# Contiguous Fourier products, an unread tile dropped and a new instruction plan in a fused attention and Fourier kernel

## The chip, the cores and the metric

The kernel runs on one core of one Trainium2 chip. The metric is the time of one execution on the device, in microseconds (us). One execution per kernel was also recorded by the profiler; its span, from the first to the last recorded instruction, is one or two us shorter than its time. A run is counted as slow when it is over 1.5% above the fastest run of the same kernel, and as fast otherwise; comparisons here are between fast runs. The engines are called as the profile calls them: PE is TensorE's matmuls and PEld its weight loads, DVE is VectorE, ACT ScalarE, POOL GpSimd, and SP the engine that issues the DMAs here.

## The reference, cut to what matters

```python
# x: 2048 x 640, 32 heads of 20, 4 segments of L = 512 tokens
q, k, v = x @ wq, x @ wk, x @ wv
for s in range(4):
    p   = softmax(q_s @ k_s^T * scale + mask)         # causal inside the segment
    num = phi(q_s) @ M;  den = phi(q_s) @ z           # memory of the segments before; M = 0 in segment 0
    o_s = g * num/den + (1 - g) * (p @ v_s)
    M += phi(k_s)^T @ v_s;  z += sum(phi(k_s))
a = o @ wo
b = irfft2(rfft2(x) * (w_r + 1j * w_i))               # over tokens and channels
return gate * a + (1 - gate) * b                      # gate = sigmoid(sum(x * gate_w))
```

phi(t) is t + 1 for positive t and exp(t) otherwise. The memory is empty in segment 0, so nobody needs phi(q) there; the full-array copy of q that phi reads is made per segment and 128-channel tile.

## The kernel before

The kernel does not fix the order of its instructions in its source. It makes some 2,350 operations, each with the buffers it reads and writes and with an assumed duration, and a list scheduler, run when the kernel is built, simulates them, picks for each engine the ready operation of the lowest priority number, and so fixes what each engine executes and in which order. On the chip every engine executes its list in that order: two profiles of the kernel after, `after` and `after_again`, show the same 3,243 matmuls in the same sequence. `PLAN` is a tuple of one correction to the priority per group of operations, found by a search against that same simulation. The chip never sees the simulated times, only the order. We call the simulation the model, and a time that it gives a planned time; none of these is a measurement.

The D products (a real Fourier transform over the channels, as matmuls with cosine and sine tables) write the even and odd frequencies to every other column of one PSUM bank, and one copy takes the bank to SBUF as `Bt`:

```python
# typ 0: cosines, typ 1: sines; (source block, first PSUM column, stride, columns, table column)
parts = ((0, 0, 2, 161, 0), (1, 0, 1, KD, 161), (2, 1, 2, 160, 482)) if typ == 0 else (
    (2, 1, 2, 160, 642), (3, 0, 1, KD, 802), (4, 0, 2, 161, 1123))          # KD = 321
for n_, (c, c0, st, n, tc) in enumerate(parts):
    ... matmul(ps(bank, c0, [st, n]), Ac[c], big[tc:tc+n], start=n_ == 0, stop=n_ == 2)
copy_alts(Bt.ap(typ * 322, [1, KD]), ps(bank, 0, [1, KD]))                   # on ACT or DVE
```

For each of 12 output tiles (segments 0 to 2, four each) the attention result `o`, which had been stored to the scratch `o_scr`, is loaded back transposed into one of four buffers `oT`, multiplied with `wo` on top of the gated Fourier part (`Fb`), copied to `ot` and stored. All these loads and stores are issued by SP, in one order:

```python
k4 = self.finc % 4                                  # four buffers oT, taken in turn
self.dma(oT[k4], o_scr tile, tr=True, name="oT")    # transposing load, 160 KB; waits for the buffer's last reader
for hf in range(2):
    self.mms(Fb ...)                                # gate * Fourier part, 32-row tiles of the array
    self.mms(5 products wo, oT ..., name="oproj")   # 320 columns each
    self.Sc.op(copy to ot ..., name="final")
self.dma(out tile, ot, name="st_out")
```

## Time and profile before

The median of the first three runs was 256.04 us (255.94 to 256.11). The first two lines below, from the top of the page, give the span and each engine's busy time, share of the span and number of instructions; then come the page's picture of the span in 40 equal slices (busy tenths of PE and of the granted clock), and the chain of waits that ended last, as shares of the span by engine.

```profile
span 255.2 us, 7980 instructions
PE 241.7 (95%) x3248; PEld 142.3 (56%) x3248; DVE 203.2 (80%) x556; ACT 202.8 (79%) x208; POOL 114.2 (45%) x175
...
PE   7999989997999999989989999999998999999994
PEclk9999997999999999999999999999999999999999
...
PE 78%; DVE 7%; DMA 5%; ACT 3%; SPq 2%; issue 1%; POOL 1%; ACTq 0%; DVEq 0%
```

PE is never idle for long, 78% of the chain is PE work, and the clock dips once (the 7 in `PEclk`). The waits of PE, in total us, number and longest, from the view of waits:

```profile
PE psum L590 <- DVE va L1086: 1.6, 1, 1.6
PE psum L590 <- DVE qu L600: 1.6, 3, 0.8
```

From the starts of neighbouring matmuls in the trace one can divide PE's time (249.7 us between its first and its last matmul) into four terms: plain work at the rate of undisturbed neighbours, 96 ns for each change of array mode, the excess inside stretches of half clock, and the rest, which is waits and slow steps. The division is the author's estimate; how much it puts down to half clock depends on whether the slow steps of PE at the start are counted, as they are here.

| between first and last matmul, us | before |
|---|---|
| plain steps | 204.1 |
| 208 changes of array mode | 20.0 |
| half clock | 4.1 |
| rest (waits, slow D steps) | 21.6 |

This agrees with what the Trainium skill says in "TensorE: Matmul & The Clock Gate", section "Back-to-back issue gap", for a step (columns / 2.4 + 2.5 ns, which the page calls the gap of an isolated matmul): the trace has 216 ns for 512 columns, 135 for 320 and 56 for 128.

### The profile page before, as it was taken

Reading aid. Unit: us, or ns where it says so; the run is one execution under the profiler, and the core shown is the slowest. Engines: PE = TensorE matmul, PEld = TensorE weight load, DVE = VectorE, ACT = ScalarE, POOL = GpSimd, SP = SyncE. Lnnn points to the kernel's source line nnn. Section 1 sums busy time; section 2 is a strip of 40 time slices with the busy share of each in tenths; the row PEclk is TensorE's granted clock in tenths of the full one; section 3 lists DMA queues with packets and bytes.
Section 4 is the critical chain, followed back from the end, with each engine's and each line's share of the span. In section 5 each row is a group of like instructions: output and inputs, shape, how many; then the busy total and the mean of one; then the engine's idle time right before and its main releaser. Section 6 shows DMA issues by size and latency. Waiting matters only on the chain.

```text
span 255.2 us, 7980 instructions
## 1 busy us (share of the span) xinstructions
PE 241.7 (95%) x3248; PEld 142.3 (56%) x3248; DVE 203.2 (80%) x556; ACT 202.8 (79%) x208; POOL 114.2 (45%) x175
## 2 busy tenths in 40 slices
PE   7999989997999999989989999999998999999994
PEld 2344556554666657644655566545564656456583
DVE  0799897768888999899999988989999984625543
ACT  2397599877899998999988889889889798788710
POOL 8015634433532346745255748434665432416400
PEclk9999997999999999999999999999999999999999
DMA  7996979499449356746247484213565303553223
GB/s 181 362 356 189 214 165 238 104 216 225 125 79 243 98 142 187 164 143 172 58 103 177 110 207 104 89 44 113 123 167 167 66 3 81 91 115 96 74 72 103
DMA packets 56003, 36.76 MB, mean 144 GB/s; under 512 B 31792, under 2 KB 52256, under 8 KB 55968
## 3 DMA queue, kind: packets, MB, share of 16 engines
q1 hardware_dynamic: 54272, 35.45, 55.1%
q10 hardware_dynamic: 1696, 0.82, 1.2%
q8 instruction: 25, 0.41, 0.7%
q14 instruction: 10, 0.08, 0.1%
HBM read 19.86 MB, written 9.84 MB: 116 GB/s over the span
## 4 chain that ended last, share of the span: by engine, by line
PE 78%; DVE 7%; DMA 5%; ACT 3%; SPq 2%; issue 1%; POOL 1%; ACTq 0%; DVEq 0%
PE psum L590 78%; DMA pkn<-phk 3%; ACT ex L1180 2%; SPq L619 2%; DVE Pt L1329 2%; DMA tt<-tab_tt 1%; DMA kp<-k_scr 1%; DVE va L1086 1%; DVE mem L1123 1%; POOL Yt L1334 1%; DVE Cp L600 1%; DVE G L1375 1%; ACT eo L598 1%; DVE qu L600 1%; POOL ex L1183 1%
## 5 line engine op out<-in xcount | busy, mean ns | idle before, releaser
L1180 ACT ACTIVATE ex<-psum 128x2048 bf16<-128x2048 f32 x80 | 150.3, 1879 | 19.2 <-PE psum L590 18.7
L1183 POOL TENSOR_SCALAR_AFFINE_SELECT ex<-ex 128x512 bf16<-128x512 bf16 x128 | 80.7, 648 | 111.3 <-ACT ex L1180 108.8
L590 PEld LDWEIGHTS psum<-va,ex 128*128 128x128 bf16 x1280 | 36.7, 96 | 6.7 <-issue 1.5
L590 PE MATMUL psum<-va,ex 128*128 128x21 bf16 x1280 | 38.6, 172 | 1.0 <-POOL ex L1183 0.3
L590 PE MATMUL psum<-qp,kp 20*128 20x512 bf16 (+3 forms) x512 | 31.9, 303 | 1.4 <-DMA kp<-k_scr 0.8
L590 PE MATMUL psum<-xT,wk 128*128 128x512 bf16 (+1 forms) x140 | 28.6, 381 | 1.3 <-DVE qu L600 0.8
L590 PE MATMUL psum<-xT,wq 128*128 128x512 bf16 (+1 forms) x140 | 28.3, 381 | 0.2 <-DVE Pt L1329 0.2
L590 PE MATMUL psum<-wv,xT 128*128 128x141 bf16 (+1 forms) x160 | 28.0, 306 | 0.0
L1329 DVE TENSOR_TENSOR Pt<-psum,Wt 128x642 bf16<-128x642 f32 x32 | 25.6, 821 | 2.1 <-PE psum L590 1.9
L590 PE MATMUL psum<-wo,oT 128*128 128x320 bf16 x120 | 22.1, 301 | 0.0
L590 PEld LDWEIGHTS psum<-qp,kp 20*128 20x128 bf16 x512 | 8.9, 92 | 21.4 <-ACT ex L1180 9.3
L590 PE MATMUL psum<-big,Ac 128*128 128x161 bf16 (+2 forms) x96 | 18.6, 316 | 0.7 <-DVE qu L600 0.6
L590 PEld LDWEIGHTS psum<-wv,xT 128*128 128x128 bf16 x160 | 13.2, 99 | 9.2 <-issue 1.2
L590 PE MATMUL psum<-big,Cp 128*128 128x321 bf16 (+1 forms) x96 | 17.2, 302 | 1.0 <-DVE eo L600 0.4
L1051 ACT ACTIVATE et<-qu 128x512 bf16<-128x512 bf16 x25 | 15.6, 630 | 2.7 <-DVE qu L600 2.5
L1086 DVE TENSOR_TENSOR va<-psum,ebx 128x500 bf16<-128x500 f32 (+1 forms) x32 | 15.2, 481 | 3.2 <-PE psum L590 2.3
L600 DVE CAST ot<-psum 128x320 bf16<-128x320 f32 x19 | 9.1, 490 | 10.6 <-PE psum L590 9.5
L590 PEld LDWEIGHTS psum<-xT,wk 128*128 128x128 bf16 (+1 forms) x140 | 9.8, 98 | 12.9 <-issue 2.2
L1375 DVE TENSOR_TENSOR G<-eo,psum 128x320 bf16<-128x320 f32 x32 | 14.6, 475 | 2.5 <-PE psum L590 2.4
L590 PEld LDWEIGHTS psum<-xT,wq 128*128 128x128 bf16 (+1 forms) x140 | 10.3, 98 | 11.2 <-issue 1.6
L1215 DVE TENSOR_TENSOR on<-psum,rs 128x320 bf16<-128x320 f32 x32 | 15.4, 482 | 0.3
L590 PE MATMUL psum<-tt,Yt 128*128 128x256 bf16 (+1 forms) x96 | 15.3, 276 | 0.1
(80 smaller groups left out, 360.0 us busy)
## 6 DMA issues: line engine op xcount, KB each, us to landing
tt<-tab_tt SPq DMA_DIRECT2D x16, 256.0 KB, 3.0
xsb<-in_A_x_dram SPq DMA_DIRECT2D x8, 320.0 KB, 6.8
qp<-q_scr SPq DMA_DIRECT2D x28, 80.0 KB
kp<-k_scr SPq DMA_DIRECT2D x28, 80.0 KB
o_scr<-on SPq DMA_DIRECT2D x12, 160.0 KB
out_dram<-ot SPq DMA_DIRECT2D x12, 160.0 KB
q_scr<-qu SPq DMA_DIRECT2D x6, 256.0 KB
k_scr<-qu SPq DMA_DIRECT2D x6, 256.0 KB, 2.8
```

Of the source, the lines that this page charges most:

```text
L590: h = e.matmul(o_, l_, r_, start=st, stop=sp_, **kw)
L598: alts["act"] = (lambda e: e.activation(dst(), src(), ACT.Copy), 100 + 0.833 * n, 95.0)
L600: alts["dve"] = (lambda e: e.tensor_copy(dst(), src()), 75 + 1.04 * n, 85.0)
L619: return e.dma_start(d_, s_)
L1051: self.one("act", lambda e: e.activation(et.ap(0, [1, L]), qsl(), ACT.Exp), L, [qb], [b("et", pi_)], late, name="phi_exp")
L1086: self.one("dve", lambda e: e.tensor_tensor(va.ap(i * H * VW + h0 * VW, [VW, nh], [1, DH]), self.ps(bank, 0, [DH, nh], [1, DH]), self.ebx. ...
L1123: self.one("dve", lambda e: e.tensor_tensor(self.mem.ap(i * D + q * 320, [DH, 16], [1, DH]), self.ps(bank, 0, [VW, 16], [1, DH]), dn.ap(16 ...
L1180: self.one("act", lambda e: e.activation(dst(), src(), ACT.Exp, scale=SC), 4 * width, [bank], [self.exb(s, g, j) for g, j in outs], prio - ...
L1183: self.one("pool", lambda e, g=g, j=j: e.affine_select(self.ex.ap(self.exo(s, g) + JOFF[j], [1280, 4], [1, P]), self.ex.ap(self.exo(s, g) ...
L1215: self.one("dve", lambda e, rs=rs, bank=bank, g=g: e.tensor_tensor(on.ap(80 * g, [D, 4], [DH, 4], [1, DH]), self.ps(bank, 0, [88, 4], [VW, ...
L1329: self.one("dve", lambda e, ri=ri, Pt=Pt, Wt=Wt, bank=bank: e.tensor_tensor(Pt.ap(ri * 322, [644, 2], [1, KD]), self.ps(bank, 0, [0, 2], [ ...
L1375: self.one("dve", lambda e, q=q, n2=n2, bank=bank, eo=eo: e.tensor_tensor(self.G.ap(n2 * D + 639 * q, [1 - 2 * q, 320]), eo.ap(q, [1, 320] ...
```

## The change

The intent: D products that write contiguous PSUM columns (odd frequencies first, then even ones, with the interleaving left to the copy that leaves PSUM), no q tile 0 in segment 0, which nobody reads, and a new plan, searched with a model that knows changes of array mode and has newly measured durations. The diff, cut to its core:

```diff
@@ the D products @@
-                parts = ((0, 0, 2, 161, 0), (1, 0, 1, KD, 161), (2, 1, 2, 160, 482)) if typ == 0 else (
-                    (2, 1, 2, 160, 642), (3, 0, 1, KD, 802), (4, 0, 2, 161, 1123))
+                parts = ((0, 160, 161, 0), (1, 0, KD, 162), (2, 0, 160, 484)) if typ == 0 else (
+                    (2, 0, 160, 644), (3, 0, KD, 804), (4, 160, 161, 1126))
-                        return (self.ps(bank, c0, [st, n]), ...
+                        return (self.ps(bank, c0, [1, n]), ...
-    copy_alts(Bt.ap(typ * 322, [1, KD]), ps(bank, 0, [1, KD]), KD)
+    copy_alts(Bt.ap(typ * 322 + 1, [-1, 2], [2, 161]), ps(bank, 0, [160, 2], [1, 161]), 322)
@@ the dropped tile @@
     def proj_tile(self, s, which, t, prio, xT, xb):
+        if s == 0 and which == "q" and t == 0:
+            return
@@ the scheduler's model @@
+    SWITCH = 95.0
+                    if o.mode != pe_mode:
+                        occ += self.SWITCH
+                        pe_mode = o.mode
-PECOL = 0.43
+PECOL = 1.0 / 2.4
-        cost = 700.0 + nbytes / 260.0 if tr else 580.0 if nbytes in (41088, 163840) else 430.0
+        cost = 740.0 + nbytes / 262.0 if tr else self.ISSUE.get(name, 450.0)
-        xfer = nbytes / row * (9.0 + row / 26.3) / 16 * 1.15
+        xfer = nbytes / row * (9.0 + row / 26.3) / 16 * 1.288
     ... (fixed parts and latencies of ACT, DVE and POOL work likewise)
     PLAN = ( ... every number replaced ... )
```

The remaining lines move table columns by a few places and pass the array mode to the model.

## The prediction

> **What bounds the kernel now.** TensorE. The page's first part has PE busy 241.7 of 255.2 us (95%), the two eviction engines 80% and 79%. The chain of waits is 78% PE. By stretches, PE has no gap from 200 to 245 us; from 100 to 200 us it is 95% busy and VectorE 93%. I take start-to-start times of neighbouring matmuls in the trace: a 512-column one takes 216 ns, 320 columns 135, 128 columns 56. That agrees with the Trainium skill, "TensorE: Matmul & The Clock Gate", section "Back-to-back issue gap" (columns / 2.4 + 2.5 ns). With such steps, 25 ns for the 21-column ones and 96 ns per change of array mode (below), PE's work adds up to about 224 us. The rest of the 249.7 us between its first and last matmul is some 3.3 us of half-speed warm-up, 3.0 us of slow D products, and about 19 us of waits, a half-clock window of 3.4 us among them.
>
> **What the change does to PE.**
> 1. D products. Today two of three write PSUM with a stride of two. The trace shows steps of 96, 178 and 96 ns for 161, 321 and 160 columns; at the rate of all other matmuls they would be 69, 136 and 69. The 321 one writes contiguously, so I read its 178 as backlog of the strided one ahead (once, with other matmuls between, it took 147). Contiguous halves save about 95 ns x 32 = 3.0 us. The eviction now interleaves on its way out; from PSUM it took 488 ns on VectorE and 442 ns on ScalarE, and I expect no more than 10% on that.
> 2. Dropped q tile: 5 x 216 = 1.1 us of PE, one ScalarE eviction (0.6 us), 128 KB of store.
> 3. Array modes. Going between full array and 32-row or 32-column tiles costs 94 to 101 ns over the plain step (317 against 216, 229 against 135, 152 against 56). The Trainium skill says that a change of mode drains the array ("TensorEngine Tiling (Array Packing)", "Key Properties"); the trace agrees. The trace has 208 changes, the built order of the changed kernel 191. 17 x 96 ns = 1.6 us.
>
> Together 5.7 us of PE work. Almost all of it lies on the chain; but D lies where VectorE is 93% busy, and VectorE's load barely falls (Yt sums and additions go to GpSimd, q and k evictions come: about -1 us, from built counts and durations). So 1 us may come back as waits.
>
> 4. The new plan, from a model with measured costs, should cut waits: the largest (1.6 us before a T product at 59 us, 0.8 at 38 and 111, eight over 0.3) are of the kind that a plan moves. I give it -2 us, uncertain by 3 either way; it may equally make or remove a half-clock window (1.7 us).
> The phi maximum: VectorE has it in both builds (30 operations, 281 to 380 ns), so nothing.
>
> **Sum.** 256.0 - 5.7 + 1.0 - 2.0 = 249.3 us, range 246.0 to 252.5.
>
> **What would show it.** D steps of 69, 136, 69 ns; 191 mode changes at about 96 ns; xT,wq full-array matmuls 95 in place of 100; Bt evictions still about 490 and 440 ns; waits of PE 16 to 19 us.
>
> **What would make it wrong.** D products slow because of accumulation over part-written columns, not stride; a strided eviction write costing much; the plan overfitted to its model, so that PE waits for loads or VectorE grow by over 3 us, or a second half-clock window.

## More of the kernel before

The groups that the change and the argument touch: D products, output products, then the copies of D to `Bt` on the two engines (count, then minimum, median and maximum duration in ns), and, of the tile `oT`, what PE and PEld sat idle for before the output products that read it (us, times), with the time of its loads from issue to landing. The last line covers only the loads whose landing the view can pair with their issue, 7 of the 12 here and 3 of the 12 in the kernel after:

```profile
L590 PE MATMUL psum<-big,Ac 128*128 128x161 bf16 (+2 forms) x96 | 18.6, 316 | 0.7 <-DVE qu L600 0.6
L590 PE MATMUL psum<-wo,oT 128*128 128x320 bf16 x120 | 22.1, 301 | 0.0
L600 DVE CAST Bt<-psum x17: 478/485/497, 50.0 to 170.2; 128x321 bf16<-128x321 f32 x17
L598 ACT ACTIVATE Bt<-psum x15: 435/442/453, 74.7 to 165.6; 128x321 bf16<-128x321 f32 x15
...
  issue: 1.1, 5
...
DMA to landing us min/median/max: 2.8/3.0/3.9
```

The idle time of PE before all 120 output products is 0.0 us, and no part of PEld's idle time is put down to an `oT` load: the loads had landed before they were needed. By the semaphores that all 12 loads raise, they took 2.75 to 5.47 us, 3.1 in the median.

## The result, and the profile after

The changed kernel's median was 267.7 us (266.17 to 269.02, four runs), beside 256.08 us of the kernel before on the same chip (255.94 to 257.31). The ratio is 1.0449, with a 95% interval of 1.0402 to 1.0496. All ratios here are the mean time of one kernel's fast runs over that of the other's of the same rounds, so they are not quite the ratios of the medians quoted. Against the predicted 249.3 us the kernel is slower, and 15 us above the upper end of the range.

Here are the same lines of the page for the kernel after:

```profile
span 264.4 us, 7987 instructions
PE 242.0 (92%) x3243; PEld 139.1 (53%) x3243; DVE 202.5 (77%) x552; ACT 203.3 (77%) x208; POOL 115.0 (44%) x178
...
PE   7869999899999999899989899999999799798994
PEclk9968999999999999999999979999999899889999
...
PE 47%; DVE 22%; DMA 16%; SPq 7%; ACT 4%; issue 3%; POOL 0%; ACTq 0%; DVEq 0%
```

The largest of its waits of PE, with the one for the table of the D products:

```profile
PE psum L600 <- DMA oT<-o_scr: 4.3, 3, 1.7
PE psum L600 <- ACT ex L1200: 3.6, 4, 2.0
...
PE psum L600 <- DMA big<-tab_big: 1.3, 1, 1.3
```

PE has the same busy time as before, but only 47% of the chain of waits is PE, with DVE, DMA and the SP queue in its place. `PEclk` has dips near the start, at about 155 us and twice near the end; by the records of the granted clock they are half-clock stretches of 6.8 us from 14.6 us on, and of 3.4 us from 154.6, 209.2 and 229.7 us on, where the kernel before had one of 3.4 us. The waits for `oT` are new, and those for the score exponentials `ex` grew from 0.4 to 3.6 us.

Two of the half-clock stretches follow waits for `oT`. The next fence shows the two windows around the dip at 209 us, of the view of busy times by stretches (start and end, length, busy us of PE, PEld, DVE, ACT and POOL with counts, the granted clock, the DMA share and GB/s):

```profile
205.80:209.20 3.40, 1.68 (x20) 0.66 (x13) 1.33 (x3) 2.54 (x4) 2.19 (x4) 1.00 1.01 155
209.20:212.60 3.40, 3.40 (x52) 1.99 (x51) 0.00 (x0) 1.46 (x2) 0.10 (x1) 0.50 0.24 73
```

PE is busy for 1.68 of 3.40 us, and most of the rest is one wait of 1.72 us for an `oT` load; the next 3.40 us run at a clock of 0.50. The Trainium skill describes such a clock gate in "TensorE: Matmul & The Clock Gate", section "What's actually happening": half rate "after ≥1 idle window (~3.4µs)". The trace agrees on the length and on the half rate, but the window shown here was not idle: PE was busy in half of it. How much idle time is enough the traces do not settle. The stretch at 154.6 us followed a window with 2.19 of 3.41 us busy and no wait for `oT`, while in the repeat `after_again` a window with 1.71 of 3.40 us busy, at 229.2 us, was followed by full clock.

The touched groups:

```profile
L600 PE MATMUL psum<-big,Ac 128*128 128x161 bf16 (+2 forms) x96 | 15.0, 261 | 3.5 <-DMA big<-tab_big 1.3
L600 PE MATMUL psum<-wo,oT 128*128 128x320 bf16 x120 | 23.2, 322 | 4.3 <-DMA oT<-o_scr 4.3
L610 DVE CAST Bt<-psum x19: 508/520/529, 54.2 to 172.5; 128x322 bf16<-128x322 f32 x19
L608 ACT ACTIVATE Bt<-psum x13: 533/538/568, 53.2 to 178.7; 128x322 bf16<-128x322 f32 x13
...
  DMA oT<-o_scr: 9.5, 6
...
DMA to landing us min/median/max: 3.2/3.4/4.3
```

D takes 3.6 us less busy time, but its copy takes 538 ns in place of 442 on ACT (22% more) and 520 in place of 485 on DVE (7% more). And PE's idle time before the output products is now 4.3 us, all of it put down to three waits for `oT` loads (the 9.5 us in six times are these and 5.2 us in three times of PEld). By the semaphores the 12 loads took 2.77 to 6.15 us, 4.3 in the median; the slower ones are not among the three of the last line.

The same division, again an estimate:

| between first and last matmul, us | before | after | difference |
|---|---|---|---|
| plain steps | 204.1 | 203.0 | -1.1 |
| changes of array mode (208, 191) | 20.0 | 18.3 | -1.6 |
| half clock | 4.1 | 7.6 | +3.5 |
| rest (waits, slow D steps) | 21.6 | 30.2 | +8.6 |
| sum | 249.7 | 259.1 | +9.4 |

So PE's plain steps and mode changes fell by 2.7 us and its D steps as shown above, and waits and half clock took 12 us. The chain of waits between 214 and 245 us of the kernel after shows how the end of the new order works (start us, length us, what):

```profile
221.90 0.41 DVE ot L610
222.31 0.02 issue
222.33 0.58 SPq L629
222.91 0.05 issue
222.96 0.55 SPq L629
223.51 0.04 issue
223.55 6.15 DMA oT<-o_scr
229.70 0.05 issue
229.75 7.30 PE psum L600 x56
237.05 4.38 DMA oT<-o_scr
241.43 0.04 issue
241.48 3.66 PE psum L600 x80
```

SP issues in order. Two output stores, which wait for copies to `ot`, stand ahead of an `oT` load (at 222.33 and 222.96 us); the load can only be issued at 223.55, lands 6.15 us later, and PE starts its products 0.05 us after that. The page "DMA: Bandwidth & Descriptors" of the Trainium skill says, in its section "Anatomy of one DMA — SWDGE (gpsimd) path", that a wait for a semaphore happens on the issuing sequencer before dispatch. The section is about another way of issuing, but the trace of these DMAs of SP agrees: the load is issued 0.04 us after the second store, and whatever stands behind a waiting DMA in SP's list waits too.

### The profile page after: what moved, and what is told of

The parts are those of the page before. It is cut to its first block, busy times and chain, and to the rows that moved or that the text cites. A ratio compares the mean times of both kernels' runs of the same rounds, so it can differ in the third digit from the quotient of the medians.

```text
span 264.4 us, 7987 instructions
## 1 busy us (share of the span) xinstructions
PE 242.0 (92%) x3243; PEld 139.1 (53%) x3243; DVE 202.5 (77%) x552; ACT 203.3 (77%) x208; POOL 115.0 (44%) x178
## 4 chain that ended last, share of the span: by engine, by line
PE 47%; DVE 22%; DMA 16%; SPq 7%; ACT 4%; issue 3%; POOL 0%; ACTq 0%; DVEq 0%
PE psum L600 47%; DMA oT<-o_scr 6%; DVE Pt L1350 4%; SPq L629 4%; DVE qu L610 3%; DMA k_scr<-qu 3%; SPq L627 3%; ACT ex L1200 2%; DMA xT<-in_A_x_dram 2%; DMA o_scr<-on 2%; DVE Yt L1355 1%; DMA gbc<-g_scr 1%; DVE G L1396 1%; DVE Cp L610 1%; DVE Bt L610 1%
## 5 line engine op out<-in xcount | busy, mean ns | idle before, releaser
L1203 POOL TENSOR_SCALAR_AFFINE_SELECT ex<-ex 128x512 bf16<-128x512 bf16 x128 | 82.4, 662 | 125.7 <-ACT ex L1200 102.0
L600 PE MATMUL psum<-qp,kp 20*128 20x384 bf16 (+3 forms) x512 | 32.5, 308 | 4.0 <-ACT ex L1200 3.6
L600 PE MATMUL psum<-xT,wk 128*128 128x512 bf16 (+1 forms) x140 | 30.9, 400 | 0.4 <-DMA xT<-in_A_x_dram 0.4
L600 PE MATMUL psum<-xT,wq 128*128 128x512 bf16 (+1 forms) x135 | 27.2, 380 | 0.9 <-ACT q L608 0.3
L600 PE MATMUL psum<-wo,oT 128*128 128x320 bf16 x120 | 23.2, 322 | 4.3 <-DMA oT<-o_scr 4.3
L600 PE MATMUL psum<-big,Ac 128*128 128x161 bf16 (+2 forms) x96 | 15.0, 261 | 3.5 <-DMA big<-tab_big 1.3
L610 DVE CAST qu<-psum 128x512 bf16<-128x512 f32 x22 | 14.9, 683 | 3.7 <-DMA k_scr<-qu 1.6
L600 PEld LDWEIGHTS psum<-wv,xT 128*128 128x128 bf16 x160 | 12.6, 97 | 9.0 <-issue 1.9
L600 PEld LDWEIGHTS psum<-wo,oT 128*128 128x128 bf16 x120 | 11.0, 103 | 11.7 <-DMA oT<-o_scr 5.2
```

What stands on the lines that cost most here:

```text
L600: h = e.matmul(o_, l_, r_, start=st, stop=sp_, **kw)
L610: alts["dve"] = (lambda e: e.tensor_copy(dst(), src()), 67 + 1.04 * n, 68.0)
L1203: self.one("pool", lambda e, g=g, j=j: e.affine_select(self.ex.ap(self.exo(s, g) + JOFF[j], [1280, 4], [1, P]), self.ex.ap(self.exo(s, g) ...
```

## The experiments

The theory that the runs were made to test is that the new order leaves its loads no slack, at the end above all, so that PE waits for DMAs, and that these waits throw it into half clock as well. Its rivals: the contiguous D products with their slower copies are what lost; dropping the tile hurts, because it shifts things; VectorE, the busiest engine beside PE in the middle, limits the new order; the losses are spread over the whole new order, and the end only collects them. The expectations call some of these by letters or "rival"; the text here names them in words. Runs of one batch shared a chip and their runs of the kernel before, whose median was 256.2 to 256.6 us in every batch. Different batches ran on different chips, so a difference of times from two batches is rougher than one from a single batch.

### The two edits without the new order, and the new order without D

`oldorder_D` keeps the order of before, instruction by instruction, and only makes D contiguous. `oldorder_D_drop` also leaves out the tile. `neworder_stridedD` is the kernel after with strided D products, its order untouched. `after_again` is the kernel after.

```diff
 # oldorder_D and oldorder_D_drop: before.py with the diff's D lines; the scheduler, its model and PLAN as in before
+        if s == 0 and which == "q" and t == 0:            # oldorder_D_drop only
+            self.Sc.gone = set(self.Sc.ops[n_ops:])       # scheduled as before, then not emitted
 # neworder_stridedD: after.py with before's table, parts and copy; model, durations and PLAN as in after
```

> The instruction order of before, kept exactly; only the D products are written in two contiguous halves and their eviction interleaves. Theory A (the edits are worth what they were costed at, the new order loses the time): D steps of 69, 136, 69 ns, 3.0 us of matmul work less, time 252.5 to 254.5 us. Rival B (the contiguous D or its interleaving eviction is what costs, the order is innocent): over 258 us, or Bt evictions much longer than 490 and 440 ns.

> The order of before, with contiguous D and the first q tile of segment 0 left out, everything else in its place. Theory A: 4.1 us of matmul work less than before, and about 1 us less than the run with D alone: 251.0 to 253.5 us. Rival B (leaving the tile out disturbs the start): no better than the run with D alone, or over 258 us.

> The changed kernel with its own order kept exactly, but the D products strided as before. Theory A: D steps go back to 96, 178, 96 ns and the time rises by 1 to 4 us over the changed kernel (268 to 272 us), so the order costs some 16 us. Rival B: it falls to 258 us or less.

> The changed kernel unchanged, for the same rounds as the three others: 266 to 269 us, three to four half-clock windows of TensorE, waits for the oT loads near 209, 230 and 241 us into the span. If these waits are chance, they lie elsewhere in this profile.

| run | median us (range) | ratio to before (95%) |
|---|---|---|
| oldorder_D | 256.51 (254.34 to 257.45) | 0.9974 (0.991 to 1.0038) |
| oldorder_D_drop | 254.18 (253.79 to 254.9) | 0.9902 (0.9848 to 0.9956) |
| neworder_stridedD | 264.17 (263.96 to 268.44) | 1.0281 (1.0229 to 1.0334) |
| after_again | 267.11 (266.39 to 268.71) | 1.0407 (1.0348 to 1.0466) |

`after_again` met its expectation: it has half-clock stretches at 17.5, 109.7 and 212.1 us, and its waits for `oT` end at 210.4, 231.3 and 242.0 us, so these are not chance. The stretches are only in part at the places of the first profile.

The edits themselves gain 2.5 us (0.98% of 256.4); the new order costs 12.9 us (267.11 less 254.18). That rules out both edits as the cause of the slowdown: with them and the old order the kernel is faster than before. The part of the D products was smaller than predicted, though: alone they gained 0.7 us (0.26%), with an interval that includes no gain. `oldorder_D` missed the expected 252.5 to 254.5 us in three of four runs, and `oldorder_D_drop` missed 251.0 to 253.5 by 0.7. Under the new order the contiguous D products even seem to cost 3 us (267.11 against 264.17). In that trace PE's D steps are slower by 2.2 us in sum than in the trace after, as they should be with strides, so it makes up for this and more elsewhere. The two traces have the same matmuls in the same sequence and differ by 0.2 us at most up to some 141 us; then `after` falls back by 2 us between 141 and 159 us, where it ran at half clock for 3.4 us (from 154.6 on) and the strided profile did not. `after_again` has no half clock there, so this stretch belongs to the one execution and not to the D edit. The expected 268 to 272 us was missed, with three of four runs near 264 and one, 268.44, counted as slow, and so was the rival's 258 or less.

### Taking away single waits of the new order

The kernel after has three groups of large waits: at the head, for score exponentials (k projections whose weights have landed stand behind score units); before the first D, for its table; and at the end, for `oT`. `new_head` and `new_big` move operations within one engine's list and leave all else; `new_tail` also adds three buffers and moves in three lists:

```diff
 # new_head: ten k projections ahead of two score units
+        ('pe', 'proj', 0, 10, ('qk', 2, 0)),
 # new_big: the table load 5 us earlier
+        ('sp', 'ld_big', 0, 1, ('ld_W', 1, 0)),
 # new_tail: seven oT buffers in place of four, three loads earlier, and PE's and ACT's order at one place
+        self.oT = [TL(f"oT{i}", [P, 5 * P]) for i in range(7)]
+        ('sp', 'oT', 6, 1, ('st_out', 1, 0)),
+        ('sp', 'oT', 8, 1, ('st_out', 3, 0)),
+        ('sp', 'oT', 9, 1, ('st_out', 3, 0)),
+        ('pe', 'oproj', 10, 5, ('Db', 66, 0)), ('act', 'exp', 66, 1, ('final', 2, 0)),
 # new_all: all of these; new_head_big: the first two
```

> The changed kernel, its order kept, but ten k projection matmuls of the start moved ahead of two score units that wait for ScalarE while the projections' weights have already landed. Theory A (the new order holds a few places with no slack, each paid in full): the TensorE waits of 1.2 and 2.0 us at 13 to 17 us and the half-clock window there go, 2 to 5 us faster than the changed kernel (262 to 265 us). Rival C (the start's delay is caught up later, since later places wait for loads anyway): within 1 us of it.

> The changed kernel, its order kept, but the load of the table for the D products issued some 5 us earlier. Theory A: the 0.8 to 1.3 us wait at 52 us goes, 0.5 to 2 us faster (265 to 267 us). Rival C: no difference.

> The changed kernel, its order kept, except at the end: seven oT buffers in place of four, three oT loads issued one to three places earlier, and one tile of output projections behind two other groups. Theory A: the three waits for oT loads (4.3 to 4.9 us together) fall below 1 us, the half-clock windows at 209 and 229 us go, 4 to 8 us faster than the changed kernel (259 to 263 us). Rival C (TensorE then waits for something else as long): less than 2 us faster.

> All three edits together. Theory A: 7 to 13 us faster than the changed kernel, 254 to 260 us, no more than two half-clock windows, so the loss of the new order sits in these five places. Rival D (the new order is worse everywhere, in many small waits behind VectorE): over 262 us.

| run | median us (range) | ratio to before (95%) |
|---|---|---|
| new_head | 264.98 (264.76 to 265.94) | 1.0327 (1.0274 to 1.0381) |
| new_big | 264.41 (262.77 to 266.44) | 1.0302 (1.0223 to 1.038) |
| new_tail | 267.49 (265.56 to 269.15) | 1.0413 (1.0319 to 1.0507) |
| new_all | 268.25 (267.95 to 270.38) | 1.0465 (1.0398 to 1.0532) |

Head and table gave some 2 us each (`new_head` as expected, but with a half-clock stretch still at 20.4 us; `new_big` a little more than expected), the tail nothing, and all three together nothing. The theory of missing slack, as it was put down, failed here, and the rival of spread losses gained. But the trace of `new_tail` shows that the edit had not taken a wait away. It had exchanged it. Its view of PE's waits has none for `oT` any more, but this one, which the kernel after does not have:

```profile
PE psum L632 <- DVE ot L642: 3.8, 1, 3.8
```

SP's timeline from 222 us on (start us, length us, line, what, count) shows why:

```profile
222.61 1.18 SPq L661 DMA_DIRECT2D out_dram<-ot  x2
223.84 10.38 SPq L659 DMA_TRANSPOSE oT<-o_scr  x3
234.25 1.72 SPq L661 DMA_DIRECT2D out_dram<-ot  x3
```

Three loads, one of them waiting for its buffer, hold SP for 10.38 us; the stores behind them are late, so the buffer `ot` stays full and the copy out of PSUM, and then PE, wait for it.

### Cutting the dependence, and lightening VectorE

`new_head_big_no_oT` gives a wrong result: on top of `new_head_big` the output products read `wo` in place of `oT`, so that nothing waits for these loads, which are still made. `new_light` and `old_light`, also wrong, cut short three kinds of VectorE work (the phi minimum, the memory addition and the fold of x), in the new and the old order.

```diff
 # new_head_big_no_oT
-    return (self.ps(bank, 0, [1, 320]), oT.ap(c * P, [1, P]), self.wo.ap(...
+    return (self.ps(bank, 0, [1, 320]), self.wo.ap(c * P, [1, P]), self.wo.ap(...
 # new_light, old_light (two of three lines)
-    fmin = lambda e: e.tensor_tensor(dst(), dst(), et.ap(0, [1, L]), ALU.min)
+    fmin = lambda e: e.tensor_tensor(few(), few(), et.ap(0, [1, 32]), ALU.min)
-    on.ap(80 * g, [D, 4], [1, 80]), on.ap(80 * g, [D, 4], [1, 80]), self.mem.ap(80 * g, [D, 4], [1, 80]), ALU.add)
+    on.ap(80 * g, [D, 4], [1, 8]), on.ap(80 * g, [D, 4], [1, 8]), self.mem.ap(80 * g, [D, 4], [1, 8]), ALU.add)
```

> The changed kernel with the two edits that gained (ten projections moved up at the start, the D table loaded earlier), without the tail edit, which only changed a wait for oT loads into a wait for output buffers. Theory A (single places without slack, each paid in full): the gains of 2.1 and 2.7 us add up, 261 to 263.5 us. Theory D (the new order stands too close behind VectorE all along, so what is gained early is lost to the next such wait): 263.5 us or more.

> Wrong result on purpose: the same, and the output projections read weights that lie in memory in place of the oT tiles, so nothing waits for oT loads (they are still issued). Theory A: another 4 to 8 us less, 254 to 258 us, close to the old order's 254. Theory D: 259 us or more.

> Wrong result on purpose: the changed kernel, order kept, with three VectorE steps cut short (phi minimum on 32 of 512 columns, addition of the memory term on a tenth, second stage of the fold on 16 columns); some 20 us of VectorE and GpSimd time less. Theory D: it gains much more than the old order does from the same cut, 8 us or more (under 259 us). Theory A: VectorE is not where the new order loses; it gains no more than the old order does.

> Wrong result on purpose: the old order with contiguous D and the tile dropped, with the same VectorE steps cut short. Theory D: the old order has slack behind VectorE, so it gains less than the new one, 0 to 4 us (250 to 254 us). Theory A says nothing against a larger gain.

| run | median us (range) | ratio to before (95%) |
|---|---|---|
| new_head_big | 267.27 (265.9 to 269.31) | 1.039 (1.0312 to 1.0468) |
| new_head_big_no_oT | 258.69 (258.16 to 259.63) | 1.0078 (1.0016 to 1.014) |
| new_light | 264.34 (263.16 to 266.0) | 1.0299 (1.0224 to 1.0373) |
| old_light | 254.62 (253.55 to 256.61) | 0.9924 (0.9843 to 1.0006) |

`new_head_big_no_oT` is 8.6 us faster (267.27 less 258.69), just above its expected 254 to 258 us. Not all of that is the waits for `oT`: the edit also frees the loads from waiting for a buffer's last reader, and in the two profiles (spans of 267.5 and 257.3 us, same matmuls in the same sequence) the first output product starts at 200.9 and 195.9 us, so that about half of the difference there arises before any output product. Lighter VectorE work gives 2.8 us in the new order, between what its two theories expected, and nothing clear of noise in the old, just above its expected 250 to 254: VectorE is not the main cause.

The single gains of head and table do not add up (`new_head_big` is no faster than `after_again`), as the theory of spread losses had expected. Where they went is visible in one profile only, that of its slowest run: its first D product comes 3.2 us earlier than in `after` (49.5 against 52.7 us), its last one 3.8 us later (181.0 against 177.2), and between them lie half-clock stretches of 6.8 us at 79.3 and of 3.4 us at 110.0 us. So in that run the gain was lost before the end; why, stays open.

### Correct kernels that test the same: the new order with slack, the old order without

A wrong kernel may hide more than the wait. So two correct ones followed. `new_tail12` has twelve `oT` buffers, five of them in the space of `wk`, which is dead by then; the first eleven loads are issued early, ahead of the stores. `new_tail12_head_big` adds the two early edits. `old_oT_late` is the inverse: `oldorder_D_drop` with two of the loads moved later in SP's list.

```diff
 # new_tail12
+        self.oT = [TL(f"oT{i}", ...) for i in range(7)] + [T(f"oT{7 + i}", [P, 5 * P], at=self.wk.off + i * 1280) for i in range(5)]
+        ('sp', 'oT', 5, 1, ('pad_k', 31, 1)),             # numbers 6 to 10 follow directly
+        ('sp', 'oT', 11, 1, ('st_out', 2, 1)),
+        ('pe', 'oproj', 10, 5, ('Db', 66, 0)), ('act', 'exp', 66, 1, ('final', 2, 0)),
 # old_oT_late, on oldorder_D_drop
+        ('sp', 'oT', 5, 1, ('st_out', 2, 1)),
+        ('sp', 'oT', 6, 1, ('st_out', 3, 1)),
```

> The order of after, result correct, but twelve oT buffers in place of four (five of them in the space of wk, which is dead by then), the first eleven oT loads issued early, ahead of the output stores, so that no load waits for a buffer's last reader and no store stands behind a waiting load; the group of output products moves with them. Theory A (the end loses some 8 us because the new plan leaves oT loads no slack, with four buffers and an in-order queue): the waits of L600-type output products on oT (4.3 us in after) vanish without the store wait that took their place in new_tail, and the time falls to 257 to 262 us. Rival (the loss is spread over the whole new order, and the end only collects it): the waits vanish but the time stays at 264 us or above, as new_tail did.

> new_tail12 plus the two earlier edits together (ten k projections ahead of two score units; the table load 5 us earlier). Theory A: once the end has no barrier of loads, what the head and the table gain is kept: 255 to 260 us, near the 258.7 us of the run whose products waited for no oT at all. Rival: 264 us or above, no better than new_head or new_big alone.

> The inverse test: the order of before with both D and drop edits (oldorder_D_drop, 254.2 us), only that two of the oT loads are issued later, number 5 behind the second output store and number 6 behind the third. Theory A: the end of the old order then shows waits of the output products on oT as after does, and the time rises by 3 to 6 us, to 257 to 260 us. Rival (oT loads are not what the new order lost by): the time stays within 1 us of 254.2 us, at most 255.5.

`new_tail12` took 260.76 us (258.41 to 261.82), ratio 1.014 (1.0064 to 1.0215), as expected. In its profile the first output product starts at 196.7 us, as in `after`, and the last at 246.2 in place of 252.2 us: the whole difference of the two profiles, 6.0 us, lies at the end, and PE waits for no `oT` load. `new_tail12_head_big` had two fast runs, 256.81 and 260.33 us (ratio 1.0067, 0.9953 to 1.018; 255 to 260 us were expected), and two counted as slow. `old_oT_late` had two fast runs, 260.31 and 261.78 us, and two counted as slow; no ratio with an interval came out of so few, but both are over 5 us above every run of `oldorder_D_drop`, and just above the upper end of what was expected. Its largest wait of PE is one wait alone:

```profile
PE psum L634 <- DMA oT<-o_scr: 5.9, 1, 5.9
```

Its chain of waits around that place (start us, length us, what):

```profile
219.26 0.54 SPq L663
219.81 0.04 issue
219.85 4.20 DMA oT<-o_scr
224.05 0.05 issue
224.10 10.93 PE psum L634 x87
```

Again a store stands ahead of a load, the load takes 4.2 us to land, and PE starts 0.05 us behind it, as in the kernel after. Beside the profile of `oldorder_D_drop` the first output product starts at the same time (201.5 and 201.4 us) and the last at 247.4 in place of 239.7 us: 7.7 us are lost there. So moving two issues in SP's list, and nothing else, costs the old order some 7 us (mean of the two fast runs, 261.0, less 254.2, of different batches), and a new order whose loads have slack wins back some 6.4 us (267.11 less 260.76, of different batches, both with 256.2 to 256.6 us for before) with a correct result. The rival of spread losses is refuted for about half of the loss. For the other half (260.8 against 254.2 us) it stands: by the plain steps the head of the new order still has some 12.6 us of PE work between 10 and 30 us where the old order with the same edits has 17.1, and the remaining waits are many and small.

### Plans chosen for slack

If missing slack made the new plan bad, then a plan of the same kind of model, but chosen for slack, should be good. For `replan_slack` the old order with both edits was improved by moving operations within each engine's list, and judged by the mean planned time over six sets of assumed durations, of which four had every load landing up to 2 us later than modelled. In the model the nominal time fell from 253.4 to 245.1 us and the worst of the six from 271.6 to 251.6 us. `replan_slack2` went on from there with eight sets, and `replan_slack2_stridedD` is the same order with the strided D products and the copies of before, to measure the first term of the prediction under a plan in which little is waited for.

```diff
+    QUEUES = {"pe": (... operation numbers in order ...), "act": ..., "dve": ..., "pool": ..., "sp": ...}
+    def relist(self):                                     # on oldorder_D_drop, ahead of the emission
+        at = {o.id: o for o in self.order}
+        seq = {e: [at[i] for i in q] for e, q in self.QUEUES.items()}
+        ... merge the five lists again, each operation after what it depends on ...
```

> Both edits of the change (D products in halves, tile dropped), result correct, but a plan of its own: the old order, improved by moving instructions within each engine's queue and judged by the mean over six sets of assumed durations, four of them with every load landing up to 2 us later than modelled. In that model the old order needs 253.4 us with nominal durations and 271.6 us in the worst set, this one 245.1 and 251.6 us (estimates of a model, not measurements). Theory A (a plan gains on the chip what it gains in the model if its loads have slack, so a correct plan with both edits beats before): 247 to 252 us, no output product waits for oT by over 0.3 us in all. Rival (the model is too rough, any plan made on it loses on the chip as after did): 256 us or above.

> replan_slack, its plan searched further with eight sets of assumed durations in place of six, result correct. In the model the nominal time is the same (245.2 us), the mean over the eight sets 1.6 us less than that of the plan of replan_slack (248.9 against 250.5 us, estimates of a model). Theory A (slack is what a plan gains by on the chip): 249 to 252 us, no half-clock stretch after the start, ratio to before 0.970 to 0.985. Rival (replan_slack was a lucky plan, a second plan of the same kind falls back): 254 us or above.

> The same order as replan_slack2, but the D products write with stride two as in before, and their copies are the shorter ones of before. If PE's steps are what the D edit is worth where PE limits, as predicted (95 ns for each of 32): 2 to 3 us slower than replan_slack2. If the copies, longer by some 96 ns on ScalarE and 34 on VectorE, take most of it back, as under the old order (0.7 us gained): at most 1 us slower. Under the order of after the strided kernel was faster by 3 us; if that were the D edit's doing and not the order's, this run is faster than replan_slack2.

| run | median us (range) | ratio to before (95%) |
|---|---|---|
| replan_slack | 251.03 (249.96 to 252.06) | 0.9813 (0.9754 to 0.9872) |
| replan_slack2 | 250.63 (249.05 to 253.46) | 0.9758 (0.9724 to 0.9791) |
| replan_slack2_stridedD | 251.42 (251.22 to 251.81) | 0.9806 (0.9781 to 0.9832) |

All three are correct. Both plans for slack beat the kernel before and the one after; `replan_slack2` is 2.4% faster than before. On the chip `replan_slack` gained some 3 us over `oldorder_D_drop` (254.18 less 251.03, of different batches) of the 8.3 us that the model promised, so the part of its theory that a plan gains on the chip what it gains in the model missed. And no plan was searched in the same way for the nominal time alone, so that slack, and not the other start and kind of search, made these plans good is argued, not shown. In the profiled execution of `replan_slack` PE waits for no `oT` load, and the page's picture of the span shows PE busy to the end and no dip of the clock:

```profile
PE   7989979999999999999989999999999999999993
...
PEclk9999999999999999999999999999999999999999
```

One of six runs of `replan_slack2`, 253.46 us, counted as slow, and it is the one that was profiled. It shows the same illness once, in small: PE waits 2.5 us for `oT`, and the clock dips near the end (at 222.4 us), where no half-clock stretch was expected. This line of its waits of PE says so:

```profile
PE psum L743 <- DMA oT<-o_scr: 2.5, 2, 2.3
```

The mean of its five fast runs is 250.18 us, and that of the strided kernel 251.42. So the D edit is worth 1.2 us under this plan (the intervals of the two ratios overlap slightly, so this size is uncertain by some 1 us). The first reading of the expectation, 2 to 3 us, missed, and so did the second, at most 1 us, by little. The third, that the edit costs time as it had seemed to under the order of after, is refuted here.

## Why the prediction was wrong, point by point

**What bounds the kernel** was read right. PE does bound the kernel before, and a plan without avoidable waits, `replan_slack2`, comes out at 250.6 us with the very edits that the prediction costed.

**Term 1, the D products, -3.0 us.** The mechanism was right and the size off. The steps became 69 to 80, about 140 and 69 to 80 ns, as predicted, and D's busy time fell from 18.6 to 15.0 us. But the copies grew by 96 ns on ACT (22%, where the prediction said "no more than 10%") and 35 on DVE (7%). In time the edit was worth 0.7 us under the old order and 1.2 us under the plan for slack. The strides slow matmuls, as the Trainium skill has it: "SBUF — State Buffer", section "Door 1: The DMA port swizzle", says that "any non-contiguous PSUM access pattern significantly slows down matmuls", and the trace's 96 ns in place of 69 for 160 columns agree. That the time did not follow the steps fits copies that become longer between D and the products that read `Bt`, but no run changed the copy alone, so this is argued, not shown.

**Term 2, the dropped tile, -1.1 us.** Full-array `xT,wq` matmuls went from 100 to 95. The step from `oldorder_D` to `oldorder_D_drop` was 1.8 us by the ratios (0.9974 less 0.9902, times 256.4), with intervals that overlap, and the two profiled spans differ by 0.3 us (252.5 and 252.2); a gain of the predicted size fits, but is not shown.

**Term 3, the array modes, -1.6 us.** 208 changes became 191, at 96 ns, so PE's work fell by 1.6 us as predicted. The Trainium skill's "TensorEngine Tiling (Array Packing)", section "Key Properties", says that a change of mode drains the array. This part came with the new order, and its worth in time was not measured by itself.

**"4. The new plan, from a model with measured costs, should cut waits ... I give it -2 us, uncertain by 3 either way"** is the step that failed. Its inverse was true: the new order costs 12.9 us against the old order with the same edits, term 3's gain already taken off. About half of that is shown to be the loads of `oT`, whose slack the new plan had used up. In the old order the output products wait 0.0 us for them; in the new one PE starts 0.05 us after a load lands, four buffers and an in-order list of issues chain each load to the last reader of a buffer and to the stores before it, and each of the two waits of 1.7 us was followed by a half-clock stretch (in the repeat, one of two). Giving the loads slack in the new order won 6.4 us, taking it away from two loads in the old order cost some 7 us. The other half, the thin head and many small waits, is shown to belong to the new order, but not to one cause.

The prediction did name this under what would make it wrong: "the plan overfitted to its model, so that PE waits for loads or VectorE grow by over 3 us, or a second half-clock window". The error was to leave it out of the sum: the prediction took a measured model for a safe one. The simulation, which was at hand, could have told. With the new durations it gives 253.4 us for the old order and 247.2 us for the new one, so it promised 6 us. With all loads 1 us later than modelled it gives 259.2 for the old and 265.9 for the new order, and with 2 us 270.3 and 299.4 (estimates of the model, with both edits; a second replay of the same lists, written apart from the first, gave 257.8 and 263.6, then 267.7 and 288.1): the sign turns, as it did on the chip, where the spans were 252.2 and 264.4 us. On the chip the load behind two stores was used 6.15 us after its issue (6.13 in the repeat).

**The check list.** Of what the prediction said would show its steps, the D steps, the 191 mode changes and the 95 full-array `xT,wq` matmuls came true. The copies and "waits of PE 16 to 19 us" did not: half clock and rest together grew from 25.7 to 37.8 us.

## What to carry to other kernels

An order that was fixed from a model is only as good as its slack: before trusting one, make all loads in the model 1 to 2 us late and see what the planned time does, and choose the plan by the mean over several such cases rather than by the nominal time; here plans made so, from the old order, gained 2.4% where the new order lost 4.5%, though a plan made the same way without the late loads was not tried. In a queue that issues in order, a store that waits for a copy, or a load that waits for a free buffer, holds up all that stands behind it, so add buffers and move issues together, and look after each edit whether the wait is gone or has only changed its name. Cost an edit and a new order separately, and measure them separately: the edits were worth 2.5 us, the order had been worth five times as much in the other direction.

## What the Trainium skill lacked or had wrong

- "TensorE: Matmul & The Clock Gate", "What's actually happening", gives half rate after an idle window of some 3.4 us, and the table under "Why this matters for your kernels" asks for no PE gaps over some 3 us. Here half-clock stretches of 3.4 us followed windows in which PE was busy for 1.68 of 3.40 us, 1.84 of 3.55 and 1.40 of 3.40; the longest single wait in the first two was 1.72 us. Another followed 2.19 of 3.41 us busy, and one window with 1.71 of 3.40 busy, in `after_again`, was followed by full clock. The page's section "A second HAM failure mode: psum-queue depth-cycling" has frequent short idles make the clock oscillate, but gives no share of a window.
- The same page, "Back-to-back issue gap", says that a stream of weight loads and matmuls is spaced by some 131 ns at 512 columns and some 81 at 128, and calls columns / 2.4 + 2.5 the isolated gap. The streams in this trace, with a weight load per matmul, step by 216 and 56 ns, which is that formula; the page's Part 1 also has about these values for matmuls back to back, so the page differs with itself.
- "SBUF — State Buffer", "Door 1: The DMA port swizzle", lets a stride of up to 8 bf16 elements go free. The copies from PSUM that write bf16 with a stride of two (and read two runs of 161 columns) took 538 ns in place of 442 on ScalarE and 520 in place of 485 on VectorE. Which of the two, the write or the split read, costs it was not separated.
- The same section says that non-contiguous PSUM access slows matmuls, without a size: 160 columns at a stride of two stepped by 96 ns in place of 69, and the contiguous matmul after them by 178 in place of some 140.
- "TensorEngine Tiling (Array Packing)", "Key Properties", says that a change of mode drains the array, without a size: 94 to 101 ns each here, 20 us of 255 in the kernel before.
- "DMA: Bandwidth & Descriptors" gives some 2.0 us as the fixed cost of one DMA, for another way of issuing, and no page has a figure for a transposing load behind other transfers. The transposing loads of 160 KB here took 3.1 us (median of 12, kernel before) and, one of them directly behind two stores of 160 KB, 6.15 us from issue to use.
